# A stack of cross layers on one core: loading and transposing x0 before the bias, and a planned order for the output transposes

## The chip, the core and the metric

The kernel runs on one core of a Trainium2 chip. The metric is the device time of one execution in microseconds (us), as the median of several. Most of what follows is read from profiles: one traced execution each, whose span (140.7 us for the kernel before) is about 1.8 us shorter than the time that is measured for the same execution (142.54 us). Engine names: PE is the matmul engine, DVE the vector engine, ACT the scalar engine, SP the engine whose queue issues the DMAs.

## The reference

```python
B, F, D, L = 1024, 26, 32, 6
Din = min(F * D, 1024)          # 832
# x0 [1024, 832], ws [6, 832, 832], bs [6, 832], all bf16

def reference(x0, ws, bs):
    x = x0
    for l in range(ws.shape[0]):
        x = x0 * (x @ ws[l] + bs[l]) + x
    return x
```

## The kernel before

The kernel keeps x transposed (features on partitions, batch rows along the free dimension), so that a layer is `w^T @ xT`. The 832 features are six chunks of 128 and one of 64; the batch is two halves (h) of 512. That gives 14 items (m, h) per layer. An item goes through three engines:

- PE: six 128-row matmuls and one 64-row matmul into one of six PSUM banks;
- ACT: adds the bias and moves the bank to SBUF;
- DVE: multiplies by x0, then adds the old x.

Each engine has one in-order queue, and semaphores connect them. Three parts matter here.

**The head.** x0 arrives with rows on partitions and has to be transposed on PE, in four batches g of 256 rows. Seven warm-up matmuls on zeros come first, then seven tiny transposes of the bias, then x0:

```python
@block.sync
def _(sp):
    for g in range(NG):                       # NG = 4
        sp.dma_start(x_in[:, 2*g : 2*g+2, :], ...).then_inc(sem_xin[g], 16)
        if g == 1:
            dma_w(sp, 0, w0_pieces[0][0], w0_pieces[0][1], sem_w0[0])   # 128 columns
            sp.dma_start(stage_b[0:L, 0:D], bst[:, :]).then_inc(sem_bias_dma, 16)
            sp.dma_start(stage_b[0:L, D:DPB], bst[:, D6:D]).then_inc(sem_bias_dma, 16)
    ...                                       # the rest of w[0], then w[1] to w[5]

@block.tensor
def _(pe):
    ...                                       # NDUMMY = 7 warm-up matmuls
    pe.wait_ge(sem_bias_dma, 32)
    for c in range(KC):                       # KC = 7
        last = pe.transpose(psbf[:, TB0 + c*L : TB0 + (c+1)*L],
                            stage_b[0:L, c*P : (c+1)*P], ident[0:L, 0:L])
    last.then_inc(sem_pe0, 1)
    for g in range(NG):
        ...
        pe.wait_ge(sem_xin[g], 16)
        ...                                   # 12 transposes 128x128, 2 of the last 64 features
    pe.wait_ge(sem_bias, 1)                   # ACT has copied the bias out
```

**The middle.** Six layers of matmuls.

**The tail.** The last layer's results have to be transposed back. For item q of the last layer PE does four transposes T(q) into one of two PSUM slots (q mod 2), then ACT (even q) or DVE (odd q) copies the slot to `out_stage`. T(q) therefore waits for two things: DVE's result of item q, and the copy of q-2. When the program is built, a small model of the queues (`est`) decides after which matmuls T(q) is emitted, and a rule decides where the copy stands in the queue of ACT or DVE:

```python
def emit_T(q):
    wait_dve(last_base + q + 1)
    if q >= 2:
        ...                                   # wait for the copy of q - 2
    ...                                       # four transposes
    gi_place[q] = max(signaled[0] - 1, last_base + q)
```

`signaled[0] - 1` is the newest item whose matmuls were emitted, so the copy goes behind every item that PE has handed over by then.

Of the kernel before, what the change touches and what calls it, by code (L numbers as in the profile page):

```python
# [5 lines left out]
P = 128  # L6
# [10 lines left out]
def bass_standalone__dcn_v2_cross__recsys_kernel(  # L17
# [23 lines left out]
    TSLOT0 = 6  # L41
    NDUMMY = 7
    EMIT_T_AGE = 6

    x0t = x0.tensor
    wst = ws.tensor
# [38 lines left out]
    with ExitStack() as es:  # L85
# [57 lines left out]
        def oev_engine(q):  # L143
            return "act" if q % 2 == 0 else "dve"
# [53 lines left out]
# [3 lines that stand above are left out]
                sp.dma_start(  # L201
                    x_in[:, 2 * g : 2 * g + 2, :],
                    x0t[2 * g * P : (2 * g + 2) * P, :].rearrange("(j p) f -> p j f", p=P),
                ).then_inc(sem_xin[g], 16)
                if g == 1:
                    dma_w(sp, 0, w0_pieces[0][0], w0_pieces[0][1], sem_w0[0])
                    sp.dma_start(stage_b[0:L, 0:D], bst[:, :]).then_inc(sem_bias_dma, 16)
                    sp.dma_start(stage_b[0:L, D:DPB], bst[:, D6:D]).then_inc(sem_bias_dma, 16)
            for i in range(1, len(w0_pieces)):
                dma_w(sp, 0, w0_pieces[i][0], w0_pieces[i][1], sem_w0[i])  # L210
            for l in range(1, L):
                dma_w(sp, l, 0, D, sem_w[l])
            n_out = 0
            wa = 0
            wd = 0
            for (r0, r1, ca, cb, qs) in out_pieces:
                qa = [q for q in qs if oev_engine(q) == "act"]
                qd = [q for q in qs if oev_engine(q) == "dve"]
                if qa:
                    na, _ = oev_counts_upto(max(qa))  # L220
                    if na > wa:
                        sp.wait_ge(sem_oev_act, na)
                        wa = na
                if qd:
                    _, nd = oev_counts_upto(max(qd))
                    if nd > wd:
                        sp.wait_ge(sem_oev_dve, nd)
                        wd = nd
                sp.dma_start(
                    outt[r0:r1, ca:cb].rearrange("(j p) f -> p j f", p=P),  # L230
                    out_stage[:, r0 // P : r1 // P, ca:cb],
                ).then_inc(sem_out, 16)
                n_out += 1
            sp.wait_ge(sem_out, 16 * n_out)
# [16 lines left out]
        def _(pe):  # L251
# [8 lines left out]
            pe.wait_ge(sem_pe0, 1)  # L260
            pe.wait_ge(sem_pool, 2)

            pe.wait_ge(sem_bias_dma, 32)
            last = None
            for c in range(KC):
                last = pe.transpose(
                    psbf[:, TB0 + c * L : TB0 + (c + 1) * L],
                    stage_b[0:L, c * P : (c + 1) * P],
                    ident[0:L, 0:L],
                )  # L270
            last.then_inc(sem_pe0, 1)

            for g in range(NG):
                pair = (g + 1) % 3
                h = (2 * g) // JH
# [21 lines left out]
                            )  # L297
                last.then_inc(sem_pe0, 1)

            pe.wait_ge(sem_bias, 1)  # L300

            state = dict(dve_need=0, act_need=0, oev_act=0, oev_dve=0, ev_act=0, ev_dve=0)
            t_emitted = [False] * NLAST
            signaled = [0]
            waited_w = set()
            est = dict(t=0.0)
            sig_est = [None] * NITEM
            act_done_est = [None] * NITEM
            dve_done_est = [None] * NITEM
            T_done_est = [None] * NLAST  # L310

            def note_signal(idx_list):
                for idx in idx_list:
                    sig_est[idx] = est["t"]
                    prev_act = act_done_est[idx - 1] if idx > 0 else 0.0
                    prev_dve = dve_done_est[idx - 1] if idx > 0 else 0.0
                    a = max(prev_act, sig_est[idx] + 0.25) + 0.72
                    act_done_est[idx] = a
                    d = max(prev_dve, a + 0.15) + 0.95
                    dve_done_est[idx] = d  # L320

            def wait_dve(need):
                if need > state["dve_need"]:
# [46 lines left out]
            def emit_T(q):  # L370
                l, m, h = items[last_base + q]
                dst = dst_of(l)
                slot0 = (TSLOT0 + (q % 2)) * BANKW
                wait_dve(last_base + q + 1)
                if q >= 2:
                    qq = q - 2
                    na, nd = oev_counts_upto(qq)
                    if oev_engine(qq) == "act":
                        if na > state["oev_act"]:
                            pe.wait_ge(sem_oev_act, na)  # L380
                            state["oev_act"] = na
                    else:
                        if nd > state["oev_dve"]:
                            pe.wait_ge(sem_oev_dve, nd)
                            state["oev_dve"] = nd
                lastt = None
                for jj in range(JH):
                    j = h * JH + jj
                    if m < NF:
                        col = slot0 + jj * P  # L390
                        lastt = pe.transpose(  # L391
                            psbf[:, col : col + P],
                            dst[:, m * B + j * P : m * B + (j + 1) * P],
                            ident[:, :],
                        )
                    else:
                        col = slot0 + jj * H
                        r0, r1 = h * H, (h + 1) * H
                        lastt = pe.transpose(  # L399
                            psbf[:, col : col + H],  # L400
                            dst[r0:r1, X6 + jj * P : X6 + (jj + 1) * P],
                            ident[r0:r1, r0:r1],
                        )
                lastt.then_inc(sem_tp, 1)
                t_emitted[q] = True
                gi_place[q] = max(signaled[0] - 1, last_base + q)
                t0 = max(est["t"], dve_done_est[last_base + q] + 0.2)
                if q >= 2 and T_done_est[q - 2] is not None:
                    t0 = max(t0, T_done_est[q - 2] + 0.9)
                est["t"] = t0 + 0.3  # L410
                T_done_est[q] = est["t"]

            def maybe_emit_T(max_n=2, final=False):
                done_last = signaled[0] - last_base
                if done_last <= 0:
                    return
                n = 0
                for q in range(NLAST):
                    if t_emitted[q]:
                        continue  # L420
                    if q >= done_last:
                        break
                    if not final:
                        if n >= max_n:
                            break
                        ready = dve_done_est[last_base + q] + 0.1
                        if q >= 2 and T_done_est[q - 2] is not None:
                            ready = max(ready, T_done_est[q - 2] + 0.8)
                        if est["t"] < ready:
                            break  # L430
                    emit_T(q)
                    n += 1

            def bank_of(idx):
                return idx % NRING
# [32 lines left out]
            for l in range(L):  # L468
                src = src_of(l)
                wbase = l * KC  # L470
                for seg in layer_segments(l):
                    sitems = seg_items(l, seg)
                    if seg[0] == "grp":
                        ms = seg[1]
                        for (_, m, h) in sitems:
                            fulls(l, m, h, src, wbase)
                            maybe_emit_T()
                        est["t"] += 0.1
                        if len(ms) == 2:
                            ma, mb = ms  # L480
                            k6mm(l, ma, 0, src, wbase, 1)
# [54 lines left out]

        @block.scalar
        def _(act):
            act.wait_ge(sem_pe0, 2)
            act.activation(  # L540
                out=bias_all[:, 0 : KC * L], in_=psbf[:, TB0 : TB0 + KC * L], func=ACT_COPY
            ).then_inc(sem_bias, 1)
            act.wait_ge(sem_bias, 1)
            for g in range(NG):
                pair = (g + 1) % 3
                h = (2 * g) // JH
                base = pair * 2 * BANKW
                act.wait_ge(sem_pe0, 2 + g + 1)
                act.activation(  # L549
                    out=x0T[:, 4 * B : 6 * B].rearrange("p (c f) -> p c f", f=B)[  # L550
                        :, :, g * 256 : (g + 1) * 256
# [10 lines left out]
                    in_=psbf[r0:r1, base + 1536 : base + 1536 + 256],  # L562
                    func=ACT_COPY,
                ).then_inc(sem_ev_act, 1)
            done_set = set()
            for gi, (l, m, h) in enumerate(items):
                bank = gi % NRING
# [15 lines left out]
        def _(dve):  # L583
            dve.memset(zeros[:, :], 0.0).then_inc(sem_dve0, 1)  # L584
            for g in range(NG):
                pair = (g + 1) % 3
                base = pair * 2 * BANKW
                dve.wait_ge(sem_pe0, 2 + g + 1)
                dve.tensor_copy(  # L589
                    out=x0T[:, 0 : 4 * B].rearrange("p (c f) -> p c f", f=B)[  # L590
                        :, :, g * 256 : (g + 1) * 256
                    ],
                    in_=psbf[:, base : base + 4 * 256].rearrange("p (c f) -> p c f", f=256),
                ).then_inc(sem_ev_dve, 1)
# [51 lines left out]
```

## Time and profile before

| | before |
|---|---|
| median of 3 runs | 143.39 us (143.3 to 143.82) |
| traced span | 140.7 us |
| first recorded real matmul | 13.02 us |
| first matmul of the last layer | 108.89 us |
| last 64-row matmul starts | 134.04 us |
| end of the last copy | 137.39 us |

The busy shares of the page, and the chain of work that ended last by engine and line:

```profile
PE 127.8 (91%) x701; PEld 55.4 (39%) x714; DVE 76.8 (55%) x180; ACT 60.0 (43%) x101; POOL 0.7 (0%) x6
...
PE 79%; DVE 7%; ACT 4%; issue 3%; SPq 2%; DMA 2%; DVEq 0%; ACTq 0%
```

PE is the busiest engine and 79% of the chain. The Trainium skill ("Perfetto Trace Analysis", Identifying the Most-Contended Engine) warns that PE's busy share does not tell how near the kernel is to its limit; its section Optimization Strategy advises to look for the gaps on that engine and for what ends them. That is the reading here, and the gaps are at both ends.

The head, from the timeline (start, duration, engine, line, operation, operands, count, and in brackets the idle time before it and what ended it). L255 are the warm-up matmuls, L266 the bias, L286 the batches of x0, L444 the first matmuls of layer 0:

```profile
1.19 3.17 PE L255 MATMUL ps<-zeros 128*128 128x512 bf16 x7 [1.19 <-DVE zeros L584]
6.71 0.31 PE L266 MATMUL ps<-ident,stage_b 6*128 6x6 bf16 x7 [2.36 <-DMA stage_b<-in_bs_dram]
6.95 0.84 PE L286 MATMUL ps<-ident,x_in 128*128 128x128 bf16 x12
8.08 1.46 PE L286 MATMUL ps<-ident,x_in 128*128 128x128 bf16 x12
9.82 1.46 PE L286 MATMUL ps<-ident,x_in 128*128 128x128 bf16 x12
11.45 0.84 PE L286 MATMUL ps<-ident,x_in 128*128 128x128 bf16 x12
12.77 4.88 PEld L444 LDWEIGHTS ps<-x0T,w_sb 128*128 128x128 bf16 x24 [0.42 <-issue]
13.02 5.12 PE L444 MATMUL ps<-x0T,w_sb 128*128 128x512 bf16 x23 [0.50 <-ACT x0T L560]
```

The page has 714 loads and 701 matmuls: 13 matmul records are missing, that of the first real matmul among them. It began 0.21 us before the 13.02 us of the first record, where the second of the weight loads starts (12.81 us); in the four complete traces this load starts with the first matmul.

PE waits 2.36 us for ten kilobytes of bias. The same 12 transposes then take 0.84 us in the first and the last batch and 1.46 us in the two between. The view by stretches shows why. Its columns are the stretch in us, its length, busy us and count of each engine, then PEclk, the granted clock:

```profile
7.00:8.00 1.00, 1.00 (x15) 0.80 (x14) 0.00 (x0) 0.21 (x1) 0.00 (x0) 0.87 1.05 396
8.00:9.00 1.00, 1.00 (x11) 0.93 (x10) 0.69 (x1) 0.75 (x2) 0.00 (x0) 0.50 1.10 353
...
11.00:12.00 1.00, 1.00 (x15) 0.71 (x14) 0.45 (x1) 0.45 (x1) 0.00 (x0) 0.93 1.10 338
```

The clock was at half from 7.73 to 11.15 us, one record of 3.413 us. The Trainium skill ("TensorE: Matmul & The Clock Gate", Part 1) says that PE's clock follows how busy PE was in the window before, that the window is 3413 ns long, and that it runs freely instead of starting with the kernel. The record's length agrees. In the window before it, 4.32 to 7.73 us, PE was busy for 1.05 us of 3.41.

The tail, from PE's timeline. L391 are output transposes:

```profile
119.51 0.39 PE L391 MATMUL ps<-ident,xTa 128*128 128x128 bf16 x4
121.73 0.38 PE L391 MATMUL ps<-ident,xTa 128*128 128x128 bf16 x4 [1.83 <-DVE out_stage L165]
122.17 1.24 PE L444 MATMUL ps<-xTb,w_sb 128*128 128x512 bf16 x5
...
130.70 0.40 PE L391 MATMUL ps<-ident,xTa 128*128 128x128 bf16 x4
132.43 0.38 PE L391 MATMUL ps<-ident,xTa 128*128 128x128 bf16 x4 [1.34 <-DVE out_stage L165]
```

T(3) and T(9) wait for the copies of items 1 and 7. On DVE's timeline the copy of item 1 (L165) stands behind all items up to 5, each a multiplication (L603) and an addition (L610). Item 5 and the copy:

```profile
120.25 0.42 DVE L603 TENSOR_TENSOR ubuf<-tbuf,x0T 64x512 bf16<-64x512 bf16 x1
120.70 0.42 DVE L610 TENSOR_TENSOR xTa<-ubuf,xTb 64x512 bf16<-64x512 bf16 x1
121.16 0.42 DVE L165 COPY out_stage<-ps 128x512 bf16<-128x512 bf16 x1
```

### The profile page before, as it was taken

What the parts mean: (1) busy time and instruction counts of PE and PEld (TensorE: products, weight loads), DVE (VectorE), ACT (ScalarE), POOL (GpSimd) and SP (SyncE); (2) the same over time, 40 slices, a digit from 0 to 9 for tenths busy, and PEclk for the clock granted to TensorE, in tenths of its full rate; (3) what the DMA queues carried; (4) which work ended last, traced back from release to release, by engine and by line L of the source; (5) the groups of instructions that cost most, each with busy time, mean ns of one, the idle gap of its engine ahead of it and who ended that gap; (6) DMA issues with size and microseconds to landing.
All of it is one profiled execution on the core that took longest, in us unless ns stands there. A gap on an engine that the chain in (4) does not pass through costs nothing.

```text
span 140.7 us, 1961 instructions
## 1 busy us (share of the span) xinstructions
PE 127.8 (91%) x701; PEld 55.4 (39%) x714; DVE 76.8 (55%) x180; ACT 60.0 (43%) x101; POOL 0.7 (0%) x6
## 2 busy tenths in 40 slices
PE   6398999999999999999999999999999999499650
PEld 2085433434343334334343433444343435234320
DVE  0034044748483667548384845775384848628830
ACT  3046060646246090615453360906245447147350
POOL 1000000000000000000000000000000000000000
PEclk9959999999999999999999999999999999999995
DMA  4999999999000000000000000000000000070046
GB/s 151 262 347 331 320 341 334 311 322 294 21 5 2 0 2 0 0 0 5 0 0 0 0 0 0 5 0 0 0 2 0 0 5 0 0 186 0 0 149 149
DMA packets 13888, 12.47 MB, mean 89 GB/s; under 512 B 4530, under 2 KB 13880, under 8 KB 13880
## 3 DMA queue, kind: packets, MB, share of 16 engines
q1 hardware_dynamic: 13880, 12.37, 29.5%
q8 instruction: 5, 0.08, 0.3%
q14 instruction: 3, 0.02, 0.1%
HBM read 10.66 MB, written 1.70 MB: 88 GB/s over the span
## 4 chain that ended last, share of the span: by engine, by line
PE 79%; DVE 7%; ACT 4%; issue 3%; SPq 2%; DMA 2%; DVEq 0%; ACTq 0%
PE ps L444 62%; PE ps L458 6%; PE ps L510 5%; DVE ubuf L603 3%; DVE xTa L610 3%; ACT tbuf L572 3%; PE ps L286 3%; DMA stage_b<-in_bs_dram 2%; PE ps L521 1%; DVE out_stage L165 1%; PE ps L391 1%; PE ps L293 1%; SPq L201 1%; ACT x0T L549 0%; SPq L182 0%
## 5 line engine op out<-in xcount | busy, mean ns | idle before, releaser
L572 ACT ACTIVATE tbuf<-ps,bias_all 128x512 bf16<-128x512 f32 (+1 forms) x84 | 51.2, 687 | 62.9 <-PE ps L458 62.8
L603 DVE TENSOR_TENSOR ubuf<-tbuf,x0T 128x512 bf16<-128x512 bf16 (+1 forms) x84 | 35.7, 424 | 45.2 <-ACT tbuf L572 38.4
L444 PE MATMUL ps<-xTb,w_sb 128*128 128x512 bf16 x209 | 48.3, 379 | 0.5 <-issue 0.2
L444 PE MATMUL ps<-xTa,w_sb 128*128 128x512 bf16 x140 | 31.9, 379 | 0.2
L444 PEld LDWEIGHTS ps<-xTb,w_sb 128*128 128x128 bf16 x216 | 20.1, 98 | 25.3 <-issue 2.8
L444 PEld LDWEIGHTS ps<-xTa,w_sb 128*128 128x128 bf16 x144 | 13.6, 98 | 17.7 <-issue 2.1
L610 DVE TENSOR_TENSOR xTa<-ubuf,xTb 128x512 bf16<-128x512 bf16 (+1 forms) x42 | 17.8, 424 | 1.4
L444 PE MATMUL ps<-x0T,w_sb 128*128 128x512 bf16 x70 | 15.8, 379 | 0.6 <-ACT x0T L560 0.5
L610 DVE TENSOR_TENSOR xTb<-ubuf,xTa 128x512 bf16<-128x512 bf16 (+1 forms) x28 | 11.9, 424 | 1.0
L444 PEld LDWEIGHTS ps<-x0T,w_sb 128*128 128x128 bf16 x72 | 6.8, 98 | 9.1 <-issue 1.3
L391 PE MATMUL ps<-ident,xTa 128*128 128x128 bf16 x48 | 4.3, 219 | 4.4 <-DVE out_stage L165 3.6
L589 DVE COPY x0T<-ps 128x1024 bf16<-128x1024 bf16 x4 | 2.8, 691 | 9.4 <-PE ps L293 9.4
L163 ACT ACTIVATE out_stage<-ps 128x512 bf16<-128x512 bf16 (+1 forms) x7 | 3.9, 564 | 5.5 <-PE ps L399 3.1
L610 DVE TENSOR_TENSOR xTb<-ubuf,x0T 128x512 bf16<-128x512 bf16 (+1 forms) x14 | 5.9, 424 | 0.5
L458 PE MATMUL ps<-xTb,w_sb 64*128 64x512 bf16 x36 | 6.0, 382 | 0.0
L391 PEld LDWEIGHTS ps<-ident,xTa 128*128 128x128 bf16 x48 | 3.0, 97 | 6.3 <-DVE xTa L610 4.0
L286 PE MATMUL ps<-ident,x_in 128*128 128x128 bf16 x48 | 4.6, 266 | 0.0
L510 PE MATMUL ps<-xTb,w_sb 128*64 128x512 bf16 x36 | 4.5, 383 | 0.0
L255 PE MATMUL ps<-zeros 128*128 128x512 bf16 x7 | 3.2, 630 | 1.2 <-DVE zeros L584 1.2
L165 DVE COPY out_stage<-ps 128x512 bf16<-128x512 bf16 (+1 forms) x7 | 2.8, 403 | 2.3 <-PE ps L399 1.1
L286 PEld LDWEIGHTS ps<-ident,x_in 128*128 128x128 bf16 x48 | 3.7, 121 | 0.5 <-issue 0.3
L458 PE MATMUL ps<-xTa,w_sb 64*128 64x512 bf16 x24 | 3.6, 381 | 0.0
(33 smaller groups left out, 25.6 us busy)
## 6 DMA issues: line engine op xcount, KB each, us to landing
w_sb<-in_ws_dram SPq DMA_DIRECT2D x5, 1248.0 KB, 11.4
x_in<-in_x_dram SPq DMA_DIRECT2D x4, 416.0 KB, 4.1
w_sb<-in_ws_dram SPq DMA_DIRECT2D x10, 104.0 KB, 10.7
out_dram<-out_stage SPq DMA_DIRECT2D x2, 512.0 KB, 3.3
w_sb<-in_ws_dram SPq DMA_DIRECT2D x1, 672.0 KB, 5.5
w_sb<-in_ws_dram SPq DMA_DIRECT2D x1, 384.0 KB, 4.8
out_dram<-out_stage SPq DMA_DIRECT2D x3, 128.0 KB, 2.8
out_dram<-out_stage SPq DMA_DIRECT2D x1, 256.0 KB, 2.7
```

The costliest lines, as they stand in the source:

```text
L163: eng.activation(out=dst_ap, in_=src_ap, func=ACT_COPY).then_inc(sem_oev_act, 1)
L165: eng.tensor_copy(out=dst_ap, in_=src_ap).then_inc(sem_oev_dve, 1)
L255: ins = pe.matmul(ps[:, NRING - 1, :], lhsT=zeros[:, 0:P], rhs=zeros[:, 0:NB], start=True, stop=True,)
L286: last = pe.transpose(psbf[:, col : col + P], x_in[:, j, c * P : (c + 1) * P], ident[:, :],)
L391: lastt = pe.transpose(psbf[:, col : col + P], dst[:, m * B + j * P : m * B + (j + 1) * P], ident[:, :],)
L444: pe.matmul(ps[:, bank, :], lhsT=w_sb[:, wbase + k, m * P : (m + 1) * P], rhs=xreg(src, k, h), start=(k == 0), stop=False,)
L458: ins = pe.matmul(ps[:, bank, :], lhsT=w_sb[r0:r1, wbase + NF, m * P : (m + 1) * P], rhs=xreg(src, NF, h), start=False, stop=True,)
L510: pe.matmul(ps[h * H : (h + 1) * H, bank, :], lhsT=w_sb[:, wbase + k, D6:D], rhs=xreg(src, k, h), start=(k == 0), stop=False,)
L572: act.activation(out=tbuf[r0:r1, gi % NT, :], in_=ps[r0:r1, bank, :], func=ACT_IDENT, bias=bias_all[r0:r1, m * L + l : m * L + l + 1], sca ...
L589: dve.tensor_copy(out=x0T[:, 0 : 4 * B].rearrange("p (c f) -> p c f", f=B)[:, :, g * 256 : (g + 1) * 256], in_=psbf[:, base : base + 4 * 2 ...
L603: dve.tensor_tensor(out=ubuf[r0:r1, :], in0=tbuf[r0:r1, gi % NT, :], in1=xreg(x0T, m, h, rows=(r0, r1)), op=ALU_MULT,).then_inc(sem_dva, 1)
L610: dve.tensor_tensor(out=xreg(dst, m, h, rows=(r0, r1)), in0=ubuf[r0:r1, :], in1=xreg(src, m, h, rows=(r0, r1)), op=ALU_ADD,).then_inc(sem_ ...
```

## The change

Three parts:

1. all of x0 is loaded before the first weights and the bias;
2. the bias transposes leave PE's head and stand inside layer 0, before the 64-row matmuls of the first group; ACT copies the bias there too, and the wait for it goes from the main loop to the first output transpose (it shares a PSUM bank with the bias);
3. in the last layer, two fixed lists replace the rules: PLAN_T says at which point between PE's matmuls T(q) is emitted, PLAN_GI behind which item its copy stands on ACT or DVE.

The diff, cut to its core (the model behind the old rule was also rewritten, but in the new kernel it no longer decides anything: both lists are constants):

```diff
+    PLAN_T = [2, 3, 4, 4, 6, 6, 8, 9, 10, 10, 11, 11, 11, 12]
+    PLAN_GI = [2, 3, 5, 4, 6, 5, 9, 9, 12, 10, 13, 12, 13, 13]
 ...
-                if g == 1:
+                if g == NG - 1:
                     dma_w(sp, 0, w0_pieces[0][0], w0_pieces[0][1], sem_w0[0])
                     sp.dma_start(stage_b[0:L, 0:D], bst[:, :]).then_inc(sem_bias_dma, 16)
 ...
-            pe.wait_ge(sem_bias_dma, 32)
-            for c in range(KC):
-                last = pe.transpose(...)          # bias
-            last.then_inc(sem_pe0, 1)
 ...
-            pe.wait_ge(sem_bias, 1)
 ...
+                if not state["bias"]:             # in emit_T
+                    pe.wait_ge(sem_bias, 1)
+                    state["bias"] = 1
 ...
-                gi_place[q] = max(signaled[0] - 1, last_base + q)
+                gi_place[q] = last_base + PLAN_GI[q]
 ...
-                    if not final:
-                        ...                        # the model's estimate of readiness
-                    emit_T(q)
+                    if not t_emitted[q] and PLAN_T[q] <= slot[0]:
+                        emit_T(q)
+                slot[0] += 1
 ...
+                        if l == 0 and ms == [0, 1]:
+                            pe.wait_ge(sem_bias_dma, 32)
+                            for c in range(KC):
+                                last = pe.transpose(...)
+                            last.then_inc(sem_pe0, 1)
```

More of the change, by code (lines that the diff above doesn't have):

```diff
@@ L261, in _ @@
             pe.wait_ge(sem_pool, 2)
-            pe.wait_ge(sem_bias_dma, 32)
-            last = None
-            for c in range(KC):
-                last = pe.transpose(
-                    psbf[:, TB0 + c * L : TB0 + (c + 1) * L],
-                    stage_b[0:L, c * P : (c + 1) * P],
-                    ident[0:L, 0:L],
-                )
-            last.then_inc(sem_pe0, 1)
             for g in range(NG):
@@ L298, in _ @@
                 last.then_inc(sem_pe0, 1)
-            pe.wait_ge(sem_bias, 1)
-            state = dict(dve_need=0, act_need=0, oev_act=0, oev_dve=0, ev_act=0, ev_dve=0)
+            state = dict(dve_need=0, act_need=0, oev_act=0, oev_dve=0, ev_act=0, ev_dve=0, bias=0)
             t_emitted = [False] * NLAST
@@ L307, in _, with recompute @@
             sig_est = [None] * NITEM
-            act_done_est = [None] * NITEM
-            dve_done_est = [None] * NITEM
             T_done_est = [None] * NLAST
+            streams = {"act": [], "dve": []}
+            done_est = {"act": [None] * NITEM, "dve": [None] * NITEM}
+            oev_done_est = [None] * NLAST
+            ACT_ITEM, DVE_ITEM, ACT_EVAC, DVE_EVAC = 0.72, 0.97, 0.62, 0.40
+            def recompute():
+                for eng in ("act", "dve"):
+                    free = 0.0
+                    for ent in streams[eng]:
+                        if ent[0] == "item":
+                            i = ent[1]
+                            if eng == "act":
+                                ready = sig_est[i] + 0.25
+                                dur = ACT_ITEM
+                            else:
+                                ready = done_est["act"][i] + 0.15
+                                dur = DVE_ITEM
+                            free = max(free, ready) + dur
+                            done_est[eng][i] = free
+                        else:
+                            q = ent[1]
+                            ready = T_done_est[q] + 0.12
+                            dur = ACT_EVAC if eng == "act" else DVE_EVAC
+                            free = max(free, ready) + dur
+                            oev_done_est[q] = free
             def note_signal(idx_list):
@@ L314, in note_signal, with place_evac, T_ready_time @@
                     sig_est[idx] = est["t"]
-                    prev_act = act_done_est[idx - 1] if idx > 0 else 0.0
-                    prev_dve = dve_done_est[idx - 1] if idx > 0 else 0.0
-                    a = max(prev_act, sig_est[idx] + 0.25) + 0.72
-                    act_done_est[idx] = a
-                    d = max(prev_dve, a + 0.15) + 0.95
-                    dve_done_est[idx] = d
+                    streams["act"].append(("item", idx))
+                    streams["dve"].append(("item", idx))
+                recompute()
+            def place_evac(q):
+                eng = oev_engine(q)
+                lo = last_base + q
+                hi = signaled[0] - 1
+                tT = T_done_est[q]
+                best = lo
+                for i in range(lo, hi + 1):
+                    d = done_est[eng][i]
+                    if d is not None and d <= tT + 0.05:
+                        best = i
+                gi_place[q] = last_base + PLAN_GI[q]
+                st = streams[eng]
+                pos = st.index(("item", best)) + 1
+                while pos < len(st) and st[pos][0] == "evac":
+                    pos += 1
+                st.insert(pos, ("evac", q))
+                recompute()
+            def T_ready_time(q):
+                r = done_est["dve"][last_base + q]
+                if r is None:
+                    return None
+                r += 0.2
+                if q >= 2:
+                    if not t_emitted[q - 2] or oev_done_est[q - 2] is None:
+                        return None
+                    r = max(r, oev_done_est[q - 2] + 0.15)
+                return r
             def wait_dve(need):
@@ L405, in emit_T @@
                 t_emitted[q] = True
-                gi_place[q] = max(signaled[0] - 1, last_base + q)
-                t0 = max(est["t"], dve_done_est[last_base + q] + 0.2)
-                if q >= 2 and T_done_est[q - 2] is not None:
-                    t0 = max(t0, T_done_est[q - 2] + 0.9)
+                rt = T_ready_time(q)
+                t0 = max(est["t"], rt if rt is not None else est["t"])
                 est["t"] = t0 + 0.3
                 T_done_est[q] = est["t"]
+                place_evac(q)
+            slot = [0]
             def maybe_emit_T(max_n=2, final=False):
-                done_last = signaled[0] - last_base
-                if done_last <= 0:
+                if signaled[0] - last_base <= 0:
                     return
-                n = 0
                 for q in range(NLAST):
-                    if t_emitted[q]:
-                        continue
-                    if q >= done_last:
-                        break
-                    if not final:
-                        if n >= max_n:
-                            break
-                        ready = dve_done_est[last_base + q] + 0.1
-                        if q >= 2 and T_done_est[q - 2] is not None:
-                            ready = max(ready, T_done_est[q - 2] + 0.8)
-                        if est["t"] < ready:
-                            break
-                    emit_T(q)
-                    n += 1
+                    if not t_emitted[q] and PLAN_T[q] <= slot[0]:
+                        emit_T(q)
+                slot[0] += 1
             def bank_of(idx):
@@ L478, in _ @@
                         est["t"] += 0.1
+                        if l == 0 and ms == [0, 1]:
+                            pe.wait_ge(sem_bias_dma, 32)
+                            last = None
+                            for c in range(KC):
+                                last = pe.transpose(
+                                    psbf[:, TB0 + c * L : TB0 + (c + 1) * L],
+                                    stage_b[0:L, c * P : (c + 1) * P],
+                                    ident[0:L, 0:L],
+                                )
+                            last.then_inc(sem_pe0, 1)
                         if len(ms) == 2:
@@ L538, in _ @@
         def _(act):
-            act.wait_ge(sem_pe0, 2)
-            act.activation(
-                out=bias_all[:, 0 : KC * L], in_=psbf[:, TB0 : TB0 + KC * L], func=ACT_COPY
-            ).then_inc(sem_bias, 1)
-            act.wait_ge(sem_bias, 1)
             for g in range(NG):
@@ L547, in _ @@
                 base = pair * 2 * BANKW
-                act.wait_ge(sem_pe0, 2 + g + 1)
+                act.wait_ge(sem_pe0, 1 + g + 1)
                 act.activation(
@@ L564, in _ @@
                 ).then_inc(sem_ev_act, 1)
+            act.wait_ge(sem_pe0, 2 + NG)
+            act.activation(
+                out=bias_all[:, 0 : KC * L], in_=psbf[:, TB0 : TB0 + KC * L], func=ACT_COPY
+            ).then_inc(sem_bias, 1)
+            act.wait_ge(sem_bias, 1)
             done_set = set()
@@ L587, in _ @@
                 base = pair * 2 * BANKW
-                dve.wait_ge(sem_pe0, 2 + g + 1)
+                dve.wait_ge(sem_pe0, 1 + g + 1)
                 dve.tensor_copy(
```

## The prediction

> **What bounds the kernel now.** The page has PE busy 91% of the 140.7 us span; DVE 55%, ACT 43%. The chain of waits is PE matmuls almost unbroken from 13.02 us to 114.6 us; the change leaves that alone. What is left is the two ends.
>
> *Head.* Timeline: warm-up matmuls end at 4.36 us, then PE idles to 6.71 us, by the chain for the bias load (landing at 6.57 us). The first x0 pieces landed at about 3.7 and 5.1 us (DMA records). Granted clock by stretch from 7 to 12 us: 0.87, 0.50, 0.50, 0.50, 0.93, so half from 7.73 to 11.15. The Trainium skill ("TensorE: Matmul & The Clock Gate", Part 1) says that the clock is set by how busy PE was in the free-running window before, 3.41 us long; the records here are 3.413 us long, so the trace agrees. A batch of x0 transposes takes 1.1 us at full clock (batches 1 and 4), 1.74 us at half (2 and 3). First real matmul: 13.02 us.
>
> *Tail.* In the last layer PE stops twice at an output transpose: 1.83 us at 121.7 and 1.34 us at 132.4 (waits: "PE ps L391 <- DVE out_stage L165", 3.6 us, 3 times). The transpose waits for a PSUM slot whose evacuation was placed on DVE behind later items, 0.98 us each.
>
> **What the change does, costed.**
> 1. x0 pieces 3 and 4 go ahead of the first weight piece and the bias; at the 320 to 390 GB/s seen x0 should be in at about 7 to 7.5 us (9.8 before), the first weights at about 8, the second piece at about 10 (11.6 before).
> 2. The bias transposes leave the head. PE starts x0 at about 4.5 us with no idle window, so four batches at 1.1 us: ends at about 8.9 (12.5 before). First matmul at about 9.3 us: 3.7 us earlier. All on the chain; later weights land 12 us or more before use.
> 3. The seven bias transposes (0.31 us) and their copy come back inside layer 0, before the 64-row matmuls: 0.4 us on PE. Net head gain 3.3 us.
> 4. The planned transposes and evacuations: I walked the three in-order queues through the last layer with the trace's durations (six matmuls 1.30, transposes 0.24, ACT item 0.61, DVE item 0.98, evacuations 0.60 and 0.42 us). For the old order it ends within 0.7 us of the trace; for the new it has no PE stall over 0.1 us before the last matmul and ends 3.6 us sooner. I take 3.3 us.
>
> Sum 6.6 us: 143.39 becomes **136.8 us**, range 135.3 to 139.3. Chances: faster by over 2% 0.95, within 2% 0.04, slower 0.01.
>
> **What would show each step.** First real matmul at 9.0 to 9.8 us; clock 1.0 from 4.3 us on; no "DMA stage_b" in the chain; layer 0's first group longer by 0.3 to 0.6 us; the span from the last layer's start to the end shorter by 2.5 to 3.7 us, with PE's waits on DVE's copies under 1 us; middle layers 19.2 us each as before.
>
> **What would make it wrong.** x0 or the first weights landing after PE wants them (over 9 us), idling PE again, perhaps at half clock; the second weight piece late (wanted at about 10.6 us); ACT's item 3, now behind the first output copy, starving DVE (the walk has it 2.5 us later) so that a transpose stalls after all; a clock window falling otherwise.

## The result

| | before | after |
|---|---|---|
| median | 143.30 us (142.38 to 143.82, 15 runs) | 135.72 us (135.33 to 137.46, 12 runs) |
| ratio, 95% interval | | 0.9484 (0.946 to 0.9508) |
| traced span | 140.7 us | 133.9 us |
| first recorded real matmul | 13.02 us | 10.37 us |
| first matmul of the last layer | 108.89 us | 106.56 us |
| last 64-row matmul starts | 134.04 us | 128.02 us |
| end of the last copy | 137.39 us | 131.12 us |

Ratios in this document are the mean time of one kernel's fast runs over that of the other's in the same rounds, so they are not quite the ratio of the medians quoted. One of the 12 runs (137.46 us, at a lower clock) is slow and is left out of the ratio; a likely cause is met under head_only.

The rows of the table subtract to a ledger of the traced 6.8 us: 2.65 us up to the first matmul, minus 0.32 us given back before the last layer, 3.69 us inside the last layer (134.04 - 108.89 = 25.15 became 128.02 - 106.56 = 21.46), 0.25 us from there to the last copy, and 0.55 us from the last copy to the end. The medians differ by 7.6 us; the other 0.8 us belongs to the kernel before, whose times form two groups, as shown below.

The page after:

```profile
PE 126.7 (95%) x701; PEld 55.1 (41%) x714; DVE 76.6 (57%) x180; ACT 59.9 (45%) x101; POOL 0.7 (1%) x6
...
PE 87%; DMA 5%; DVE 2%; issue 2%; SPq 1%; DVEq 0%
```

The instructions are the same in number (1961) and PE's busy time almost so; the chain is now PE for 87% and holds no bias. The head after (L278 are the batches of x0, L475 the matmuls):

```profile
4.41 1.46 PE L278 MATMUL ps<-ident,x_in 128*128 128x128 bf16 x12
6.16 0.94 PE L278 MATMUL ps<-ident,x_in 128*128 128x128 bf16 x12
7.72 0.84 PE L278 MATMUL ps<-ident,x_in 128*128 128x128 bf16 x12 [0.40 <-DMA x_in<-in_x_dram]
9.10 0.83 PE L278 MATMUL ps<-ident,x_in 128*128 128x128 bf16 x12 [0.30 <-DMA x_in<-in_x_dram]
10.37 3.90 PE L475 MATMUL ps<-x0T,w_sb 128*128 128x512 bf16 x17 [0.21 <-issue]
```

PE starts x0 at 4.41 instead of 6.95 us, and now waits for x0 itself: the last piece landed at 8.96 us. The first batch ran at half clock (1.46 us). The granted-clock column hides that:

```profile
4.35:6.20 1.85, 1.79 (x15) 1.43 (x16) 0.00 (x0) 0.00 (x0) 0.00 (x0) 1.00 0.88 264
```

It says 1.00, but the trace's first clock record begins only at 6.39 us, and where there is no record the view counts full clock. The duration of a batch is the safer clock: 0.84 us at full, 1.46 us at half.

The tail after (L434 are the output transposes):

```profile
116.96 0.39 PE L434 MATMUL ps<-ident,xTa 128*128 128x128 bf16 x4
117.40 1.24 PE L475 MATMUL ps<-xTb,w_sb 128*128 128x512 bf16 x5
118.48 0.61 PE L434 MATMUL ps<-ident,xTa 128*128 128x128 bf16 x8
118.92 1.46 PE L475 MATMUL ps<-xTb,w_sb 128*128 128x512 bf16 x6
```

No line has a bracket: from 106.63 to 128.34 us PE is busy for 21.55 of 21.71 us. On DVE the copies (L167) now stand between the items; the copy of item 1 goes right behind item 3 and before item 4, at 117.88 us:

```profile
117.53 0.42 DVE L651 TENSOR_TENSOR xTa<-ubuf,xTb 128x512 bf16<-128x512 bf16 x1
117.88 0.42 DVE L167 COPY out_stage<-ps 128x512 bf16<-128x512 bf16 x1
118.21 0.41 DVE L644 TENSOR_TENSOR ubuf<-tbuf,x0T 64x512 bf16<-64x512 bf16 x1
```

### The profile page after: what moved, and what is told of

Its sections match the earlier page's. It is cut to its first block, busy times and chain, and to the rows that moved or that the text cites. A ratio compares the mean times of both kernels' runs of the same rounds, so it can differ in the third digit from the quotient of the medians.

```text
span 133.9 us, 1961 instructions
## 1 busy us (share of the span) xinstructions
PE 126.7 (95%) x701; PEld 55.1 (41%) x714; DVE 76.6 (57%) x180; ACT 59.9 (45%) x101; POOL 0.7 (1%) x6
## 4 chain that ended last, share of the span: by engine, by line
PE 87%; DMA 5%; DVE 2%; issue 2%; SPq 1%; DVEq 0%
PE ps L475 69%; PE ps L489 7%; PE ps L551 6%; DMA x_in<-in_x_dram 5%; PE ps L434 2%; PE ps L562 1%; SPq L203 1%; DVE xTa L651 1%; DVE ubuf L644 1%; PE ps L278 1%; DVE out_stage L167 0%; PE ps L514 0%; PE ps L285 0%; PE ps L442 0%; DVEq L643 0%
## 5 line engine op out<-in xcount | busy, mean ns | idle before, releaser
L475 PE MATMUL ps<-xTb,w_sb 128*128 128x512 bf16 x209 | 48.1, 379 | 0.5 <-issue 0.2
L475 PE MATMUL ps<-xTa,w_sb 128*128 128x512 bf16 x140 | 31.7, 379 | 0.3 <-issue 0.2
L475 PEld LDWEIGHTS ps<-xTb,w_sb 128*128 128x128 bf16 x216 | 20.2, 98 | 24.8 <-issue 2.4
L475 PEld LDWEIGHTS ps<-xTa,w_sb 128*128 128x128 bf16 x144 | 13.6, 98 | 17.7 <-issue 2.2
L475 PE MATMUL ps<-x0T,w_sb 128*128 128x512 bf16 x70 | 15.8, 379 | 0.3 <-issue 0.2
L475 PEld LDWEIGHTS ps<-x0T,w_sb 128*128 128x128 bf16 x72 | 6.7, 98 | 8.9 <-issue 0.8
L434 PE MATMUL ps<-ident,xTa 128*128 128x128 bf16 x48 | 4.2, 220 | 0.9 <-ACT out_stage L165 0.8
L585 ACT ACTIVATE x0T<-ps 128x512 bf16<-128x512 bf16 x4 | 2.4, 598 | 5.5 <-PE ps L285 5.5
L278 PE MATMUL ps<-ident,x_in 128*128 128x128 bf16 x48 | 4.1, 246 | 0.8 <-DMA x_in<-in_x_dram 0.7
L434 PEld LDWEIGHTS ps<-ident,xTa 128*128 128x128 bf16 x48 | 3.0, 97 | 2.9 <-DVE xTa L651 1.5
L278 PEld LDWEIGHTS ps<-ident,x_in 128*128 128x128 bf16 x48 | 3.3, 111 | 2.1 <-PE ps L257 1.0
L167 DVE COPY out_stage<-ps 128x512 bf16<-128x512 bf16 (+1 forms) x7 | 2.8, 404 | 1.6 <-PE ps L434 0.9
```

The costliest lines, as they stand in the source:

```text
L167: eng.tensor_copy(out=dst_ap, in_=src_ap).then_inc(sem_oev_dve, 1)
L278: last = pe.transpose(psbf[:, col : col + P], x_in[:, j, c * P : (c + 1) * P], ident[:, :],)
L434: lastt = pe.transpose(psbf[:, col : col + P], dst[:, m * B + j * P : m * B + (j + 1) * P], ident[:, :],)
L475: pe.matmul(ps[:, bank, :], lhsT=w_sb[:, wbase + k, m * P : (m + 1) * P], rhs=xreg(src, k, h), start=(k == 0), stop=False,)
```

## The experiments

Twelve kernels were run; all computed the reference's result. The theory: the head and the tail are two separate stages; in the head PE waits first for the bias and then for x0, with the half clock as a consequence of the wait; in the tail PE waits for copies that stand too late on DVE. The rivals are named in each expectation.

| kernel | median, us | ratio to before | first recorded real matmul in its trace, us | from the last layer's first matmul to the end, us |
|---|---|---|---|---|
| before | 143.30 | 1 | 13.02* | 31.8 |
| changed kernel | 135.72 | 0.9484 | 10.37* | 27.3 |
| head_only | 140.81 | 0.9854 | 12.24* | 31.8 |
| tail_only | 138.10 | 0.9669 | 13.20* | 27.3 |
| bias_only | 140.41 | 0.9815 | 10.88* | |
| order_only | 146.43 | 1.0251 | 16.74* | |
| plan_t | 141.36 | 0.9896 | 13.77 | 30.2 |
| plan_gi | 139.65 | 0.9795 | 12.69 | 28.9 |
| warm | 141.34 | 0.9900 | 11.60 | |
| after_oldloads | 135.81 | 0.9509 | 10.18 | |
| x0_alone | 140.63 | 0.9848 | 11.94* | |
| after_again | 135.77 | 0.9511 | 10.37* | |
| x0_halves | 135.75 | 0.9498 | 10.50* | |
| after_third | 135.59 | 0.9496 | 10.19* | |

The last column is the span minus the start of the last layer's first matmul, for the kernels where the tail is the question. In the traces with a * the record of the first real matmul is missing: by the weight loads it began 0.21 to 0.22 us earlier (0.39 in head_only, at half clock). Take that off before you compare them with the four others, which record every matmul.

### Each end alone: head_only and tail_only

head_only is the kernel before with parts 1 and 2 of the change, tail_only with part 3.

```diff
 # head_only, against the changed kernel: the old rules in the last layer
-                gi_place[q] = last_base + PLAN_GI[q]
+                gi_place[q] = max(signaled[0] - 1, last_base + q)
 ...                                  # and the old maybe_emit_T
 # tail_only, against the changed kernel: the old head
-                if g == NG - 1:
+                if g == 1:
+            pe.wait_ge(sem_bias_dma, 32)      # and the bias transposes, before x0
```

> The head of the change alone (x0 loads first, bias transposes inside layer 0), the last layer as before. Theory A, the two ends are independent and both gains reach the end: in the two traces the last layer's first matmul moved from 108.96 to 106.63 us, so this is 2.3 us faster than before in a trace, 2.3 to 3.2 us in the times (some runs of before lose about 0.85 us more to the clock): 140.0 to 140.9 us. Rival B, DVE and not PE sets the pace of the last layer, so an earlier start is partly lost there: under 1.5 us.

> The planned last layer alone, the head as before. Theory A: from the last layer's first matmul to the end 31.7 us became 27.3 us, so 4.4 us faster: about 138.8 us, and two groups of times 0.85 us apart stay, as in before. Rival B: the tail's gain needed the earlier head, under 3.5 us.

head_only: ratio 0.9854, about 2.1 us (2.3 to 3.2 were expected); tail_only: 0.9669, about 4.7 us (4.4 expected; one minus the ratio, times 143 us). The last column of the table is the cleaner measure of the tail, as it doesn't contain the head: 31.8 us with the old rules whatever the head, 27.3 us with the lists whatever the head. So the two ends add, and rivals B fall. The product of the two ratios is 0.9528, against 0.9484, 0.9511 and 0.9496 in the three measurements of the changed kernel. head_only's own trace is a warning: it is of its slowest run (142.15 us, the others 140.17 to 140.98 us). There x0's third piece landed at 8.65 us, PE idled for 1.61 us before it, and the clock fell again, from 9.13 to 12.54 us. That run pulls the ratio up. So the new head is not proof against the clock; a longer wait for x0 brings the half clock back. The one slow run of the changed kernel (137.46 us) and one of bias_only (142.39 us) lie as far from their neighbours, also at a lower clock, but have no trace, so that this is their cause is only argued; their mean clocks (0.984 and 0.980, where head_only's traced run has 0.983) fit it. The two groups of times stayed in tail_only only roughly (four runs from 137.96 to 138.17 us, two at 138.72 and 139.01).

### The two parts of the head: bias_only and order_only

```diff
 # bias_only, against head_only
-                if g == NG - 1:
+                if g == 1:
 # order_only, against the kernel before
-                if g == 1:
+                if g == NG - 1:
```

> The bias transposes inside layer 0 as in the change, but the loads in the old order (first weight piece and bias between x0 pieces 2 and 3, which landed at 8.6 and 9.8 us). Theory A, after the bias the landing of x0 piece 4 is what gates the first matmul: first matmul at 11.2 to 11.6 us (13.02 before, 10.37 with the whole change), 1.1 to 2.1 us faster than before. Rival C, the bias wait was everything and the load order is worth nothing: the whole 2.3 us or more.

> x0 loads first, but the bias transposes stay at PE's head. Theory A: the bias now lands at about 10.3 us, PE idles from 4.4 to 10.4 us and runs x0 transposes partly at half clock; first matmul at 16 to 17.5 us, so 3 to 4.5 us SLOWER than before: about 147 us. Rival D, the load order is where the gain is and the bias is off the path: faster than before by 1 us or more.

order_only is slower, ratio 1.0251 (theory A: 3 to 4.5 us; 143.27 to 146.43 in medians). Its timeline shows the bias, now last in line, still first on PE, and batches at half clock behind it:

```profile
9.67 0.33 PE L266 MATMUL ps<-ident,stage_b 6*128 6x6 bf16 x7 [5.32 <-DMA stage_b<-in_bs_dram]
9.93 1.46 PE L286 MATMUL ps<-ident,x_in 128*128 128x128 bf16 x12
```

bias_only was expected to give 1.1 to 2.1 us under theory A. It gave more: ratio 0.9815, about 2.6 us, no less than head_only. Its trace starts layer 0 on x0, not on the bias:

```profile
8.45 0.84 PE L276 MATMUL ps<-ident,x_in 128*128 128x128 bf16 x12 [1.97 <-DMA x_in<-in_x_dram]
...
10.88 5.13 PE L434 MATMUL ps<-x0T,w_sb 128*128 128x512 bf16 x23 [0.17 <-issue]
```

That expectation missed, and rival C was right: moving the bias is the whole of the head's gain, and the load order adds nothing that shows. after_oldloads, below, asks the same of the whole change.

### The same question in the whole change: after_oldloads

```diff
-                if g == NG - 1:
+                if g == 1:
```

> The whole change, but with the loads in the old order. Bias moved alone already gave as much as the whole head (ratio 0.9815 against 0.9854). Theory I, the load order is worth nothing once the bias is off the head: ratio to before within 0.003 of the changed kernel's 0.9484, about 135.7 us. Rival C, the new load order is worth the 0.5 us by which the first matmul was earlier in the changed kernel's trace (10.37) than in bias_only's (10.88): about 136.2 us, ratio 0.952.

Ratio 0.9509, against 0.9484, 0.9511 and 0.9496 for the changed kernel: theory I, though the ratio's interval (0.9475 to 0.9544) holds rival C's 0.952 as well. The traces decide: with the missing records counted in, the first matmul began at 10.18 us in the old order and at 10.15, 10.15 and 9.98 us in the three traces of the new one, not 0.5 us earlier. Why the order is worth nothing can be read from the landings of the DMAs. In the old order x0's last piece landed at 9.00 us here and the first weights at 6.32; in the new order, 8.96 and 10.09 us. The new order brings x0 forward by little and puts the first weights back so far that they become a second gate at the same place. In the trace of after_again PE's last wait before the first matmul is for them (0.21 us of the 0.31 is the first matmul, whose record is missing):

```profile
9.00 0.83 PE L278 MATMUL ps<-ident,x_in 128*128 128x128 bf16 x12 [0.31 <-DMA x_in<-in_x_dram]
...
10.37 5.13 PE L475 MATMUL ps<-x0T,w_sb 128*128 128x512 bf16 x23 [0.31 <-DMA w_sb<-in_ws_dram]
```

### The price of the half clock: warm

The kernel before, with nothing moved; PE is only kept busy while it waits.

```diff
-    NDUMMY = 7
+    NDUMMY = 13
```

> The kernel before with 13 warm-up matmuls instead of 7, so that PE is busy until about 5.7 to 6.9 us, while it waits for the bias anyway. Theory G, a part of the head's loss is the half clock after the idle stretch: no half-clock record between 7 and 12 us, batches 2 and 3 at 1.1 us instead of 1.74, first matmul at 11.5 to 12.1 us, about 1.1 us faster than the 143.3 us group and no second group of times. Rival H, the half clock costs nothing since x0's landing (9.8 us) gates: within 0.3 us of before.

```profile
7.22 0.84 PE L286 MATMUL ps<-ident,x_in 128*128 128x128 bf16 x12
...
10.24 0.84 PE L286 MATMUL ps<-ident,x_in 128*128 128x128 bf16 x12
11.60 3.61 PE L444 MATMUL ps<-x0T,w_sb 128*128 128x512 bf16 x16 [0.29 <-ACT x0T L560]
```

All four batches (two are shown) run at full clock, and the first matmul is at 11.60 us (theory G: 11.5 to 12.1). Ratio 0.9900, about 1.4 us, with one constant changed; the traced span is 1.21 us shorter. So half or more of what the new head gains (1.5 and 1.9% by head_only and bias_only, 2.33 us in the traces) can be had without moving the bias at all: it was the half clock that came with the waiting.

It also answers for the groups of times. The 15 runs of before lie from 142.38 to 142.86 (six) and from 143.29 to 143.82 us (nine), with nothing between; in later rounds some fall between (143.02 and 143.06 us). The six runs of warm lie within 0.42 us, and the changed kernel's fast runs within 0.7 us. plan_t, which has the head of before, was traced in another phase of the clock's window: its first full-clock record begins at 12.71 us, three batches are at half clock instead of two, and its first matmul comes 0.96 us later than in the trace of before (13.77 against 12.81 us, the missing record counted in). 0.21 us of that is the bias, which PE gets at 6.92 us here and at 6.71 us there; the clock's part is the other 0.75 us. In this phase no record shows that the clock had risen at all before the wait.

```profile
7.17 1.46 PE L287 MATMUL ps<-ident,x_in 128*128 128x128 bf16 x12
...
10.66 1.46 PE L287 MATMUL ps<-ident,x_in 128*128 128x128 bf16 x12
12.41 0.97 PE L287 MATMUL ps<-ident,x_in 128*128 128x128 bf16 x12
13.77 1.46 PE L434 MATMUL ps<-x0T,w_sb 128*128 128x512 bf16 x6 [0.16 <-issue]
```

That is about the distance of the groups. The untraced runs don't show their phase, so that each of them belongs to a phase is argued. The record supports it: of the 40 runs of before in the experiments' rounds, the 21 with spans of 140.4 to 140.8 us have a mean granted clock of 0.975 to 0.980 or of 0.996 to 0.998, the 16 with spans of 141.3 to 141.8 us have 0.989 to 0.993, and the three others (140.9 to 141.3 us) 0.986 or 0.987. That warm has one group is shown, and that another phase cost 0.75 us is seen in one pair of traces.

### The two lists of the tail: plan_t and plan_gi

Both have the head of before.

```diff
 # plan_t: where PE puts T(q) by the list, copies by the old rule
+                    if not t_emitted[q] and PLAN_T[q] <= slot[0]:
+                        emit_T(q)
 # plan_gi: T(q) by the old rule, copies by the list
-                gi_place[q] = max(signaled[0] - 1, last_base + q)
+                gi_place[q] = last_base + PLAN_GI[q]
```

> The kernel before with the planned places of the output transposes on PE alone; evacuations placed by the old rule (behind the newest signalled item). Theory A, transposes and evacuations must fit each other and each list alone gives part: the walk of the queues says 1.3 us faster than before (the full tail gave 4.4 to 5.2 us), with PE still waiting for DVE's copies about 2 us. Rival E, where PE puts the transposes is everything: 4 us or more.

> The kernel before with the planned places of the evacuations on ACT and DVE alone; PE's order as before. Theory A: the walk says 1.6 us faster than before, by DVE copying out right after the item that the transpose needs. Rival F, where the evacuations stand is everything, since PE's long waits were for DVE's copies: 4 us or more.

From the last layer's first matmul to the end: 31.8 us before, 30.2 with the transposes' list, 28.9 with the copies' list, 27.3 with both. The parts are 1.56 and 2.94 us and add to the whole, 4.50. For the transposes the walk was close (1.3 us expected); for the copies it was too low (1.6 us). Neither rival reached its 4 us. The waits of PE's transposes for DVE's copies (us in total, times, longest) in the last layer of before and of plan_t, and of plan_gi, in this order:

```profile
PE ps L391 <- DVE out_stage L165: 3.6, 3, 1.8
```

```profile
PE ps L392 <- DVE out_stage L166: 2.3, 3, 1.4
```

```profile
PE ps L392 <- DVE out_stage L166: 0.9, 1, 0.9
```

The copies' list takes away most of the waiting, since the waiting was for copies that stood behind items. What is left in plan_gi is T(3): by the old rule it comes one group of six matmuls earlier than by the list, and waits 0.87 us there.

### What keeps x0 late: x0_alone

```diff
                 if g == NG - 1:
+                    for gg in range(NG):
+                        sp.wait_ge(sem_xin[gg], 16)
```

> The whole change, but the first weights and the bias are issued only when all of x0 has landed. It asks why x0's last piece landed at 8.96 us and not at the 7 to 7.5 us of the prediction. Theory J, x0 shares the DMA engines with the weights issued behind it: alone it is in by 7.0 to 7.7 us; the first weights then land at 10 us or later and the first matmul is at 10.5 to 11.5 us, so the time is 0.2 to 1.2 us above the changed kernel's. Rival K, x0's own transfers take that long: last piece at 8.6 us or later even alone, first matmul after 11.5 us.

> The changed kernel again, beside the run above on the same chip: ratio to before 0.945 to 0.952, all its times within 0.5 us of each other, since its head no longer leaves the idle stretch that let the clock fall in some phases.

x0's last piece landed at 8.50 us even with nothing behind it. That is between the two theories, and nearer to K. In the three traces of the changed kernel it landed at 8.75 to 8.96 us, so sharing the DMA engines with the weights seems to cost x0 a quarter to half a microsecond. One trace can't tell it more closely: in the old order of loads the same piece landed anywhere from 8.93 us (warm) to 9.81 us (before). The Trainium skill ("DMA: Bandwidth & Descriptors", Why a DMA increments its semaphore by 16 and not by 1) says that a transfer is spread over up to 16 engines which finish independently, and each adds one to the semaphore. The trace has these 16 increments: for this piece twelve came from 6.67 to 7.40 us, the other four from 8.20 to 8.50. The stage ends with its slowest shares, and in the stretch from 7 to 8 us the DMA engines are busy for only a quarter of the time (columns as above, ending with clock, DMA share, GB/s):

```profile
6.00:7.00 1.00, 0.40 (x5) 0.14 (x2) 0.69 (x2) 0.85 (x4) 0.00 (x0) 1.00 0.79 296
7.00:8.00 1.00, 0.51 (x9) 0.52 (x10) 0.12 (x1) 0.29 (x2) 0.00 (x0) 1.00 0.25 97
```

The third piece's four last shares were late too (7.15 to 7.44 us, the other twelve by 6.36 us). Why four shares come late is open. The time missed its expectation too: 140.63 us, some 4.9 us above the changed kernel where 0.2 to 1.2 were expected. Two waits for weights follow, of about 2.0 us for the first piece (2.24 us up to the first recorded matmul) and 2.33 us for the second; the second had been forgotten. Its times form two groups again (139.71 and 139.82; 141.44 and 141.48 us).

### An attempt to beat it: x0_halves

```diff
+            for j in range(4, 8):             # x0's last two pieces as four, each with its semaphore
+                sp.dma_start(x_in[:, j, :], x0t[j*P : (j+1)*P, :]).then_inc(sem_xhalf[j-4], 16)
 ...                                           # the first weights before them, the bias after the second piece
-                for c in range(KC):
-                    for jj in range(2):
+                for jj in range(2):
+                    pe.wait_ge(sem_xhalf[j - 4], 16)     # g >= 2
+                    for c in range(KC):
```

> An attempt to beat the changed kernel. In every order of loads tried the last piece of x0 is in at 8.9 to 9.5 us, and after it stand 14 transposes (1.06 us) and then the first matmul (10.2 to 10.4 us). Here the last two pieces are loaded as four halves, each with its own semaphore, the transposes go half by half, and the bias is issued behind the second weight piece (it is needed at 15.4 us only). If the landing of x0's last bytes gates the start: the last seven transposes (0.53 us) follow the last half, first matmul at 9.6 to 10.0 us, 0.3 to 0.6 us under the changed kernel. If it is instead the second weight piece (in at 11.0 to 11.4 us, wanted 1.3 us after the first matmul), or the number of transfers, that gates: within 0.2 us of it or slower.

> The changed kernel once more, to be compared on the same chip with x0_halves: 135.4 to 136.0 us.

It is the same: ratio 0.9498 against 0.9496 on the same chip. The halves landed at 7.77, 8.30, 8.87 and 9.45 us, later than pieces of the changed kernel, and from 7.81 us PE transposes without a pause at 0.61 us per half until 10.34 us, so its first matmul is at 10.50. Its first weights are in at 6.24 us (9.92 in after_third), but they go ahead of these halves. The same bytes come in another order, and the start does not move. No version tried beats the changed kernel.

## Why the prediction was right or wrong

The time was right: 136.8 us forecast with a range from 135.3 to 139.3, 135.72 measured, and faster by over 2% as forecast. Two terms of its sum were mis-sized, in opposite directions, and a third was missing: 6.6 us less 1.0 in the head, plus 1.2 in the tail, plus 0.8 for the groups of times makes the 7.6 us measured. That the total came so close is in part luck.

- **The head ("3.7 us earlier", "net head gain 3.3 us").** Right mechanism, too large: 2.65 us in the trace, 2.33 us after the bias came back. The step that failed is the first, x0 "in at about 7 to 7.5 us": it landed at 8.96 us. x0_alone shows that the forecast could not have been met even without sharing (8.50 us): a rate averaged over all 16 engines doesn't tell when the slowest share is in. The first weights were put at 8 us and landed at 10.09.
- **What in the head counted.** The prediction gave the load order a part of the gain. bias_only and after_oldloads show none. The load order alone is harmful (order_only, 1.0251).
- **The half clock.** That the idle stretch caused it and that removing it would pay was right (warm, 0.9900). "Clock 1.0 from 4.3 us on" was wrong for the trace in hand, where full clock came at 6.39 us; it cost nothing there, as x0 was late anyway.
- **The bias inside layer 0 (0.4 us).** 0.32 us: in layer 0 the second group's first matmul comes 16.29 - 10.37 = 5.92 us after the first group's, against 18.62 - 13.02 = 5.60.
- **The tail (3.3 us).** Too small: 4.5 us. The walk itself had said 3.6, and the discount went the wrong way. In the traces the last copy ends 3.94 us sooner after the layer's start, and another 0.55 us is gained from there to the end; the record doesn't say whether the walk went on after the last copy. The stated sign was there: no PE stall before the last matmul, no wait for DVE's copies. ACT's third item did move behind the first copy, and DVE then sat idle for 1.22 us before item 3, but no transpose stalled for it.
- **The groups.** The 0.8 us between the median and the traced run, which the phase of the clock explains if the groups are its doing, were not in the sum. The forecast was taken from the median of 143.39 us, but the steps were read from a trace of a run in the faster group (142.54 us). The change takes away the slower group as well, and this made good most of what the head fell short of. The list of what could go wrong did name the clock's window.
- **The middle.** Layers 2 to 4 take 19.22 us each in both traces, as forecast.

## What to carry to other kernels

An instruction that waits for a tiny load and stands first in an in-order queue delays all behind it; move it to where its result is needed, and do it before touching the order of the loads, which here was worth nothing after that move and cost 2.5% without it. If an engine must wait at the start, look at what the wait does to the clock afterwards: six more dummy matmuls were worth 1% here. In an in-order tail, place each copy right behind the result that it frees a buffer for, and measure the two queues' lists separately: two thirds of this tail's gain was where the copies stood, one third where the transposes stood.

## What the Trainium skill lacked or had wrong

- "TensorE: Matmul & The Clock Gate", Part 4, says that the full clock doesn't engage for PE's transpose mode, as it doesn't count as PE being busy in the same way. Here full clock did follow windows of nothing but transposes (the profile lists them as MATMUL and doesn't show the mode): in order_only the first full-clock record begins at 15.90 us, after a window (12.49 to 15.90 us) of nothing but transposes, and the first other matmul is at 16.53 us. In the trace of before, transposes alone filled the window from 7.73 to 11.15 us, and full clock followed. Whether they count for less than other matmuls is open; the next point leaves room for it.
- The same page, Part 1, says that the clock falls after an idle window. The window need not be wholly idle: it fell after windows with PE busy, almost all of it with transposes, for 1.05 us (before) and 1.81 us (head_only) of 3.41, and stayed up after 2.11 us (after_oldloads) and 2.22 us (after_again). But busy time alone doesn't decide it. In x0_alone the clock stayed up after the window from 10.86 to 14.27 us, in which PE was busy for 1.24 us (about 1.5 with the first matmul, whose record is missing) and only with matmuls 512 columns wide. It did not rise after 2.82 us of transposes (order_only) and rose after 2.85 us of warm-up matmuls (x0_alone, 0.62 to 4.03 us).
- The same page says not to fit a model to the count of cold matmuls because the phase varies, and puts the penalty of the ramp under 1% of a typical kernel's span. It gives no figure for the phase in a kernel whose head idles: 0.75 us between two traces here, and two groups of times; 1.0% for the half clock as a whole (warm).
- "Perfetto Trace Analysis" doesn't warn that a clock column can read 1.00 where the trace has no record yet: batches of 12 transposes took 1.46 us under a printed clock of 1.00, and 0.84 us at full clock. Nor does it say that matmul records can be missing: 13 of 714 in ten of the fourteen traces here, found by counting the weight loads.
- "DMA: Bandwidth & Descriptors" says that the 16 engines finish independently, but gives no spread for loads issued from SP (a row of its "Latency and other measured facts" names two engines that are usually slower in traces, without a figure): four of the sixteen shares of x0's last piece came 0.8 us or more after the other twelve, with no weights in flight (8.20 to 8.50 against 6.67 to 7.40 us).
